# Twenty-eight more softmax tiles transposed by the DMA crossbar, a convolution without a pass for its middle tap, and a list scheduler that holds the DMA queue only while it issues

## The chip, the cores and the metric

One core of a Trainium2 chip. The metric is the device time of one execution in microseconds; lower is better. Engines: PE multiplies matrices, DVE, ACT and POOL work element by element, SP issues nearly all DMAs, in its program's order. Every engine runs its instructions in order and waits at semaphores.

## The reference

Attention with a threshold, then a gated feed-forward network, all in float32. B = 8 batches, 8 heads, S = 576 positions, head dimension 64; the model has 512 columns, the hidden layer 1024.

```python
scores = scale * np.matmul(q, k.transpose(0, 1, 3, 2))
thresh = np.max(scores, axis=-1, keepdims=True) - tau
scores = np.where(scores >= thresh, scores, -1000000000.0)
...
attn = attn / (np.sum(attn, axis=-1, keepdims=True) + 1e-09)
return np.matmul(attn, v).astype(np.float32)
...
h = np.maximum(x @ w_in, 0.0)
...
for k in range(K):
    conv_out += conv_w[k][None, None, :] * hp[:, k:k + S, :]
gate = 1.0 / (1.0 + np.exp(-conv_out))
return (h * gate @ w_out).astype(np.float32)
```

x has the heads of one position side by side. The convolution runs over positions, with three taps for each hidden column.

## The kernel before

**Tiles and stages.** The 576 positions of a batch are five tiles, four of 128 rows and one of 64. Two heads make a pair, four pairs a batch; a batch is cut into two chunks of tiles, (0, 1) and (2, 3, 4). A *unit* is one tile of one pair: 160 in all, in the order batch, chunk, pair, tile. Odd pairs take a chunk's tiles in reverse. For each unit and head PE computes the scores (`ps_s`, 128 x 576), DVE the row maximum into `few`, ACT the exponential into `em`, DVE the mask and its sum, and POOL multiplies by the inverse sum (`em`, line 602). The product with v needs the probabilities transposed. A full tile has 9 blocks of 128 x 128 (two heads of 576 columns): PE transposes 4, 4 and 1 of them into `ps_t` (line 661), the last in a group `odd` shared by the tiles of a pair, and ACT copies them to `eT` (line 656). When the last tile of an odd pair is there, `attend` multiplies `eT` of both pairs with v into `pa` (lines 716 and 725); in the first batch each pair does so alone.

**The crossbar path.** Where `crossed(i, t)` is true, `cross` does the transposing without PE: ACT and POOL split the 32-bit words of `em` into two halves of 16 bits (`parts`), SP stores them to DRAM (`rows`), and two transposing DMAs bring them back into `eT`. Before, that is the first tile of the even pairs of each chunk, except in batch 0 (`plain`): 28 tiles.

**The feed-forward part.** When the four pairs of a chunk are there, `mm1(c, f, xs)` computes 128 of the hidden columns over a chunk's positions (8 calls a chunk, 128 in all): 12 matmuls into `ph`; ACT's ReLU into `hp`, halved; the middle tap `cw[1] * hp` into `t`, on ACT for three calls of four and on POOL for the fourth (`TAP`); two DVE instructions that add the outer taps; ACT's tanh; DVE's gate `(t + 1) * hp`; and the split into the ring `g` for float32 products, which `mm2` multiplies with w_out into `po` (line 826) for 128 positions at a time.

**What sets the order.** Nothing runs where it stands in the code. `op(engine, ns, fn, ...)` puts each instruction on a list with a duration, a rank and what it reads and writes, and `Plan.run` plays the list with these durations, `LATENCY` behind each (`late` is added to it), and the counts of buffers: on each free engine the ready instruction of the lowest rank goes next, and the instructions are emitted in that order. For some operations an engine is chosen among `other`. So the durations given to SP decide where its DMAs stand among each other and how early the instructions that need them stand on other engines.

Of the kernel before, what the change touches and what calls it, by code (L numbers as in the profile page):

```python
# [10 lines left out]
F32 = mybir.dt.float32  # L11
# [4 lines left out]
AF = mybir.ActivationFunctionType  # L16
ALU = mybir.AluOpType
# [4 lines left out]
AHEAD = {'s': 6.25, 's4': 7.75, 't': 3.5, 'a': 3.5, 'prep': 4.25, 'w': 2.5, 'load': 7.75}  # L22
# [6 lines left out]

NEAR = 8  # L30
PIECES = 12
TAP = ('act', 'pool', 'act', 'act')
LOW = ('pool', 'pool')
HPB = 3
MOE = (2, 2)
# [16 lines left out]

FAR = 3
EMS = 5

KEEP = {'rows': 2.304, 'cols': 1.613, 'turn': 3.226, 'full': 2.304}

# [192 lines left out]
def tile_tau_attention_gated_ffn(  # L250
# [49 lines left out]
    def const(name, shape, dtype):  # L300
        return plan.buf(cpool, name, 1, shape, dtype, name)
# [30 lines left out]
    def sp(n):  # L332
        return 2.6 * n

    def act(n, psum=False):
        return n * 0.833 + (58 if psum else 95)

    def dve(n, fixed=65):
        return n * 1.07 + fixed
# [4 lines left out]
    def pool1(n):  # L344
        return n * 0.9 + 225
# [69 lines left out]
    cw = const("cw", [P, n3], F32)  # L415
    cwl = const("cwl", [P, n3], F32)

    def load_conv():
        split(conv_w, n3, "stage_c", lambda: cw[:], lambda: cwl[:], (cw, 0), (cwl, 0))
        op("dve", 100, lambda: nc.vector.tensor_tensor(cw[:], cw[:], cwl[:], op=ALU.add), w=[(cw, 0)], r=[(cwl, 0)])  # L420

    w1 = [const(f"w1{i}", [P, NCB, DF], F32R) for i in "hl"]
    w2 = [const(f"w2{i}", [P, NFB, DO], F32R) for i in "hl"]
# [22 lines left out]
    def plain(b):  # L446
        return b == 0
# [39 lines left out]

    def prep_k(b, p, ks):

        a = AHEAD["prep"]  # L490
        xk = plan.buf(wk, "xk", 2, [P, S + D], F32, f"xk_{b}_{p}")
        op("sp", sp(S), lambda: nc.sync.dma_start(xk[:, :S], kt[b, p]), w=[(xk, 0), (xk, 1)], ahead=a + 2)
        op("act", act(S), lambda: nc.scalar.activation(xk[:, :S], xk[:, :S], AF.Copy, scale=0.125), w=[(xk, 0), (xk, 1)], ahead=a)
        op("act", act(S), lambda: nc.scalar.activation(ks[:, 0], xk[:, :S], AF.Copy), w=[(ks, (0, 0)), (ks, (0, 1))], r=[(xk, 0)], ahead=a)
        op(
            "pool", pool(S), lambda e: subtract(e, xk[:, :S].bitcast(F32R), xk[:, :S], ks[:, 0].bitcast(F32)),
            w=[(xk, 0), (xk, 1)], r=[(ks, (0, 0)), (ks, (0, 1))], ahead=a, other=[("dve", dve(S))], port=True
        )
        halves(ks, (ks, Later(lambda: ks[:, 0], S), ((0, 0), (0, 1))), [((1, 1), 1)], a)
        halves(ks, (xk, Later(lambda: xk[:, :S].bitcast(F32R), S), (0, 1)), [((1, 0), 1), ((0, 1), 0)], a)  # L500

    def prep_q(i, b, p, q1, q2):

        w, o = QW, chunks[pairs[i][0]].new[0]
        xq = plan.buf(wk, "xq", 2, [P, w], F32, f"xq_{i}")
        a = AHEAD["prep"]
        op("sp", sp(w), lambda: nc.sync.dma_start(xq[:], qt[b, p, :, o:o + w]), w=[(xq, 0)], ahead=a + 2)
        op("act", act(w), lambda: nc.scalar.activation(q1[:, 0], xq[:], AF.Copy), w=[(q1, (0, 0)), (q1, (0, 1))], r=[(xq, 0)], ahead=a)
        op(
            "pool", pool(w), lambda e: subtract(e, q2[:, 0], xq[:], q1[:, 0].bitcast(F32)),  # L510
            w=[(q2, (0, 0)), (q2, (0, 1))], r=[(xq, 0), (q1, (0, 0)), (q1, (0, 1))], ahead=a, other=[("dve", dve(w))], port=True
        )
        for q in (q1, q2):
            halves(q, (q, Later(lambda q=q: q[:, 0], w), ((0, 0), (0, 1))), [((1, 1), 1), ((1, 0), 1), ((0, 1), 0)], a)

    def load_v(i, b, p):
        vt = plan.buf(wk, "v", 2, [P, NBLK, D], F32, f"v_{i}")
        op("sp", sp(NBLK * D), lambda: nc.sync.dma_start(vt[:], vc[b, p]), w=[(vt, 0)], ahead=AHEAD["prep"])
        return vt

    def unit(u, k, q1, q2, o, n):
# [90 lines left out]

    def crossed(i, t):
        c, p = pairs[i]
        return not plain(chunks[c].b) and p % 2 == 0 and t == order(i)[0]

    def cross(u, em, eT, off):

        parts = plan.buf(wk, "parts", 2, [P, 2, 2 * S], U16, f"parts_{u}")
        rows = plan.buf(far, "rows", FAR, [2 * P, 2 * S], U16, f"rows_{u}")  # L620
        a = AHEAD["s"]
        for j in range(2):
            def part(e, j=j):
# [9 lines left out]
        op(  # L633
            "sp", sp(2 * S), lambda: nc.sync.dma_start(rows[:].rearrange("(q two) k -> q two k", two=2), parts[:]),
            w=[(rows, 0)], r=[(parts, 0), (parts, 1)], ahead=a
        )
        for j in range(2):
            def turn(j=j):
                nc.sync.dma_start_transpose(eT[:].bitcast(U16)[:, off // D + j], rows[j * P:(j + 1) * P, :])
# [101 lines left out]
    def mm1(c, f, xs):  # L741
# [25 lines left out]
        def relu():  # L767
            nc.scalar.activation(hp[:, o:o + an], ph[:, :an], AF.Relu, scale=0.5)  # L768

        def tap0(e):  # L770
            if e == "act":
                nc.scalar.activation(t[:, :kn], hp[:, 1:kn + 1], AF.Copy, scale=cw[:, 3 * f + 1:3 * f + 2])  # L772
            else:
                engines[e].tensor_scalar(
                    t[:, :kn], hp[:, 1:kn + 1], cw[:, 3 * f + 1:3 * f + 2], 1.0, op0=ALU.mult, op1=ALU.mult
                )

        op("pool", 36, edge, w=[(hp, 1)])
        op("act", act(an, True), relu, w=[(hp, 0)], r=[(ph, 0)])
        choice = {"pool": pool1(kn), "dve": dve(kn / 2, 75), "act": act(kn)}  # L780
        home = TAP[f % len(TAP)]
        op(
            home, choice[home], tap0, w=[(t, 0)], r=[(hp, 0), (cw, 0)], port=True,
            other=[(e, ns) for e, ns in choice.items() if e != home]
        )
        for k in (0, 2):
            def tap(k=k):
                nc.vector.scalar_tensor_tensor(  # L788
                    t[:, :kn], hp[:, k:kn + k], cw[:, 3 * f + k:3 * f + k + 1], t[:, :kn], op0=ALU.mult, op1=ALU.add
                )  # L790

            op("dve", dve(kn, 150), tap, w=[(t, 0)], r=[(hp, 0), (hp, 1), (cw, 0)], port=True)

        def gate():
            nc.vector.scalar_tensor_tensor(t[:, :kn], t[:, :kn], 1.0, hp[:, 1:kn + 1], op0=ALU.add, op1=ALU.mult)  # L795

        op("act", act(kn), lambda: nc.scalar.activation(t[:, :kn], t[:, :kn], AF.Tanh), w=[(t, 0)])  # L797
        op("dve", dve(kn), gate, w=[(t, 0)], r=[(hp, 0)], port=True)

        at = (b * S + k0) % RING  # L800
# [16 lines left out]
    def mm2(m):  # L817

        gh, gl = ring
        at = m * P % RING  # L820
        po = plan.buf(ps_w, "ps_w", 2, [P, 512], F32, f"po_{m}")
        ot = plan.buf(wk, "ot", 2, [P, DO], F32, f"ot_{m}")
        for f in range(NFB):
            def mm(f=f):
                for i, (x, w) in enumerate(((gh, w2[0]), (gl, w2[0]), (gh, w2[1]))):
                    nc.tensor.matmul(  # L826
                        po[:], lhsT=x[:, f, at:at + P], rhs=w[:, f, :],
                        start=(f == 0 and i == 0), stop=(f == NFB - 1 and i == 2)
                    )
# [165 lines left out]
```

## Time and profile before

| | |
|---|---|
| median of 3 runs | 921.64 us (921.11 to 922.96) |
| the profiled execution: time, span | 924.3 us, 922.5 us |
| mean granted TensorE clock | 0.992 |
| PE busy in its span | 883.3 us, 6056 matmuls and transposes |
| DVE, ACT, POOL busy | 755.5, 699.5, 616.9 us |
| DMA | 137.0 MB, queue 1 takes 54.7% of 16 engines' time |

Busy times of the engines overlap. A row of the groups gives an instruction's line, engine and operation, what it writes and reads, the shapes and the count, then the busy time, the mean duration in ns, and how long the engine stood idle ahead of it, with who ended that. The chain follows back from the last instruction whatever released each step.

### The profile page before, as it was taken

The page shows a single profiled execution, that of the slowest core. Times are in us where ns is not written, and L with a number is a line of the kernel's source. Part 1 is how long each engine was busy: PE and PEld are TensorE (multiplying, and loading weights), DVE is VectorE, ACT ScalarE, POOL GpSimd, SP SyncE. Part 2 cuts the span into 40 slices and gives each one's busy share as a digit, 9 for nine tenths or more (in the row PEclk, how much of TensorE's full clock was granted, in tenths as well). Part 3 has the DMA queues.
Part 4 walks back from the last instruction along what each step waited for, and adds up shares of the span by engine and source line. Part 5 has one row for each costly group of instructions (what it writes and reads, how often), then busy time and mean ns, then how long its engine had stood idle before and what let it go on. Part 6 is the DMA issues. An engine that isn't in the chain of part 4 may idle for free.

```text
span 922.5 us, 19191 instructions
## 1 busy us (share of the span) xinstructions
PE 883.3 (96%) x6056; PEld 708.5 (77%) x6056; DVE 755.5 (82%) x1871; ACT 699.5 (76%) x1547; POOL 616.9 (67%) x1053
## 2 busy tenths in 40 slices
PE   5989799999999999999999999999899999999998
PEld 3546578778788787888788788887788888877896
DVE  5899799968789878896988779897888879988543
ACT  5778688768778787887878687787868868876753
POOL 3566777757768676785868767776676758775422
PEclk9999899999999999999999999999999999999999
DMA  6554357457675566547675376556757278653000
GB/s 211 174 172 133 82 149 186 128 157 162 173 186 140 153 189 189 121 121 195 177 189 153 104 193 165 137 150 169 194 150 183 75 192 195 175 135 101 24 24 34
DMA packets 148260, 137.02 MB, mean 149 GB/s; under 512 B 85312, under 2 KB 116288, under 8 KB 148160
## 3 DMA queue, kind: packets, MB, share of 16 engines
q1 hardware_dynamic: 147296, 133.90, 54.7%
q10 hardware_dynamic: 864, 1.90, 0.7%
q8 instruction: 49, 0.80, 0.4%
q14 instruction: 51, 0.42, 0.2%
HBM read 58.88 MB, written 25.95 MB: 92 GB/s over the span
## 4 chain that ended last, share of the span: by engine, by line
PE 73%; DVE 9%; POOL 6%; ACT 6%; issue 3%; DMA 3%; SPq 0%; ACTq 0%; POOLq 0%; DVEq 0%
PE po L826 20%; PE ph L753 13%; PE pa L725 13%; PE ps_s L549 11%; PE ps_t L661 10%; POOL em L602 3%; PE ps_s L542 3%; DVE em L569 3%; DVE few L557 2%; PE pa L716 2%; ACT eT L656 1%; DVE t L788 1%; ACT em L566 1%; PE pw_stage L399 1%; DMA stage<-in_w_in_dram 1%
## 5 line engine op out<-in xcount | busy, mean ns | idle before, releaser
L602 POOL TENSOR_SCALAR em<-em,few 128x576 f32<-128x576 f32 x286 | 262.7, 926 | 35.0 <-DVE few L593 21.7
L569 DVE SCALAR_TENSOR_TENSOR em<-ps_s,few,em 128x576 f32<-128x576 f32 x288 | 229.9, 813 | 26.4 <-ACT em L566 15.2
L557 DVE TENSOR_REDUCE few<-ps_s 128x1 f32<-128x576 f32 x288 | 210.1, 750 | 43.4 <-PE ps_s L549 28.0
L753 PE MATMUL ph<-x,w1h 128*128 128x322 f32 (+1 forms) x1024 | 239.0, 306 | 3.4 <-ACT hp L768 2.5
L566 ACT ACTIVATE em<-ps_s,few 128x576 f32<-128x576 f32 x288 | 208.1, 742 | 41.0 <-DVE few L557 36.8
L656 ACT ACTIVATE eT<-ps_t 128x512 f32<-128x512 f32 (+2 forms) x360 | 167.9, 487 | 30.4 <-PE ps_t L661 27.6
L788 DVE SCALAR_TENSOR_TENSOR t<-hp,cw,t 128x255 f32<-128x255 f32 (+1 forms) x256 | 160.0, 634 | 33.6 <-ACT t L772 28.6
L753 PEld LDWEIGHTS ph<-x,w1h 128*128 128x128 f32 x1024 | 174.4, 190 | 10.2 <-ACT hp L768 4.7
L661 PE MATMUL ps_t<-ident,em 128*128 128x128 f32 x1060 | 158.3, 279 | 9.7 <-POOL em L602 4.4
L549 PE MATMUL ps_s<-ks,q 128*128 128x288 f32 x896 | 152.8, 305 | 6.2 <-issue 3.8
L661 PEld LDWEIGHTS ps_t<-ident,em 128*128 128x128 f32 x1060 | 125.6, 143 | 36.9 <-POOL em L602 14.9
L753 PE MATMUL ph<-x,w1l 128*128 128x322 f32 (+1 forms) x512 | 151.6, 296 | 0.0
L549 PEld LDWEIGHTS ps_s<-ks,q 128*128 128x128 f32 x896 | 129.4, 189 | 23.3 <-issue 13.3
L329 POOL TENSOR_TENSOR gl<-t,gh 128x255 fp32r<-128x255 f32 (+9 forms) x192 | 121.0, 644 | 32.6 <-ACT gh L805 32.3
L725 PE MATMUL pa<-eT,v 128*64 128x320 f32 (+1 forms) x1024 | 132.2, 410 | 0.0
L826 PE MATMUL po<-w2h,gh 128*128 128x512 f32 x288 | 119.8, 416 | 0.6 <-ACT hp L768 0.6
L725 PEld LDWEIGHTS pa<-eT,v 128*64 128x64 f32 x1024 | 70.4, 137 | 58.9 <-issue 15.4
L826 PE MATMUL po<-w2l,gh 128*128 128x512 f32 x288 | 113.8, 395 | 0.0
L826 PE MATMUL po<-w2h,gl 128*128 128x512 f32 x288 | 113.4, 394 | 0.0
L753 PEld LDWEIGHTS ph<-x,w1l 128*128 128x128 f32 x512 | 97.1, 190 | 0.4
L795 DVE SCALAR_TENSOR_TENSOR t<-t,hp 128x321 f32<-128x321 f32 (+1 forms) x128 | 74.5, 584 | 12.6 <-ACT t L797 11.5
L563 POOL TENSOR_SCALAR few<-few,ntau 128x1 f32<-128x1 f32 x96 | 34.5, 360 | 67.0 <-DVE few L557 51.7
(72 smaller groups left out, 1106.7 us busy)
## 6 DMA issues: line engine op xcount, KB each, us to landing
q<-q SPq DMA_DIRECT2D x336, 64.0 KB, 2.1
v<-in_vc_dram SPq DMA_DIRECT2D x64, 288.0 KB, 3.6
rows<-parts SPq DMA_DIRECT2D x28, 576.0 KB, 3.4
k<-in_kp_dram SPq DMA_DIRECT2D x35, 320.0 KB, 3.8
out_dram<-ot SPq DMA_DIRECT2D x36, 256.0 KB, 2.3
xk<-in_kt_dram SPq DMA_DIRECT2D x28, 288.0 KB, 3.2
ks<-xk SPq DMA_DIRECT2D x56, 144.0 KB, 2.6
xq<-in_qt_dram SPq DMA_DIRECT2D x56, 128.0 KB, 2.5
```

Source lines behind the costliest of these rows:

```text
L329: engines[e].tensor_tensor(dst, x, y, op=ALU.subtract)
L549: nc.tensor.matmul(ps[:, c, :CH], lhsT=q[:, h, o:o + n], rhs=k[:, h, c * CH:(c + 1) * CH], start=(i == 0), stop=(i == 1))
L557: nc.vector.tensor_reduce(few[:rows, nm], ps[:rows, :, :CH], op=ALU.max, axis=mybir.AxisListType.XY, negate=True)
L566: nc.scalar.activation(view(), ps[:rows, :, :CH], AF.Exp, bias=few[:rows, nm])
L569: nc.vector.scalar_tensor_tensor(view(), ps[:rows, :, :CH], few[:rows, th], view(), op0=ALU.is_ge, op1=ALU.mult, accum_out=few[:rows, total])
L602: engines[e].tensor_scalar(sl, sl, by, to, op0=ALU.mult, op1=ALU.add)
L656: "act", act(w, True), lambda dst=dst, src=src: nc.scalar.activation(dst(), src(pt), AF.Copy),
L661: nc.tensor.transpose(out=pt[:, at:at + P], in_=em[:, int(b * P):int(b * P) + P], identity=ident[:])
L725: nc.tensor.matmul(pa[j * D:(j + 1) * D, :w], lhsT=vt[:, blk, :], rhs=eT[:, :w // D, blk, :], start=False, stop=(r == 3))
L753: nc.tensor.matmul(ph[:, :an], lhsT=w1[w][:, cb, fs], rhs=xs[cb][:, h, :an], start=(cb == 0 and i == 0), stop=(cb == NCB - 1 and i == 2))
L788: nc.vector.scalar_tensor_tensor(t[:, :kn], hp[:, k:kn + k], cw[:, 3 * f + k:3 * f + k + 1], t[:, :kn], op0=ALU.mult, op1=ALU.add)
L826: nc.tensor.matmul(po[:], lhsT=x[:, f, at:at + P], rhs=w[:, f, :], start=(f == 0 and i == 0), stop=(f == NFB - 1 and i == 2))
```

## The change

There are three parts, and the order of the whole program follows from them.

1. `crossed` takes the first full tile of every pair in each chunk but those of batch 0: 56 tiles. In odd pairs, whose order is reversed, that is tile 1 of the first chunk and tile 3 of the second.
2. The pass for the middle tap is gone. Once, from the loaded taps, 14 small DVE instructions make `cr`, the outer taps divided by the middle one, and `cm`, whose first row is the middle tap, moved a little where it is next to zero. Each call then has two DVE instructions, `hp[0] * cr0 + hp[1]` and `hp[2] * cr1 + t`, and tanh takes `cm` as its scale.
3. In the list, a load or a store holds SP for 450 ns, and the rest of its old duration is added to the time until its data is there (`put`). The small copies between partitions (`halves`) hold SP for 550 ns, a transposing DMA for 1400 with 700 behind it.

```diff
-TAP = ('act', 'pool', 'act', 'act')
...
+CROSS = (1, 1)
...
+    def put(fn, n, issue=450, **kw):
+        op("sp", issue, fn, late=max(sp(n) - issue, 0), **kw)
...
     def load_conv():
...
-        op("dve", 100, lambda: nc.vector.tensor_tensor(cw[:], cw[:], cwl[:], op=ALU.add), w=[(cw, 0)], r=[(cwl, 0)])
+        v = nc.vector
+
+        def steps():
+            yield v.tensor_tensor, (cw[:], cw[:], cwl[:]), dict(op=ALU.add)
+            for i, k in enumerate((0, 2)):
+                yield v.tensor_scalar, (cr[:, i], taps(k), -1.0, None), dict(op0=ALU.mult)
+                yield v.tensor_tensor, (cr[:, i], cr[:, i], taps(k)), dict(op=ALU.max)
...
+            yield v.scalar_tensor_tensor, (cm[:, 0], cm[:, 0], 2.0, taps(1)), dict(op0=ALU.mult, op1=ALU.add)
+            yield v.reciprocal, (cm[:, 1], cm[:, 0]), {}
+            for i, k in enumerate((0, 2)):
+                yield v.tensor_tensor, (cr[:, i], taps(k), cm[:, 1]), dict(op=ALU.mult)
...
             op(
-                "sp", max(sp(n) / 2, 360),
+                "sp", 550,
...
-        op("sp", sp(S), lambda: nc.sync.dma_start(xk[:, :S], kt[b, p]), w=[(xk, 0), (xk, 1)], ahead=a + 2)
+        put(lambda: nc.sync.dma_start(xk[:, :S], kt[b, p]), S, w=[(xk, 0), (xk, 1)], ahead=a + 2)
...
-        op("sp", sp(w), lambda: nc.sync.dma_start(xq[:], qt[b, p, :, o:o + w]), w=[(xq, 0)], ahead=a + 2)
+        put(lambda: nc.sync.dma_start(xq[:], qt[b, p, :, o:o + w]), w, w=[(xq, 0)], ahead=a + 2)
...
-        op("sp", sp(NBLK * D), lambda: nc.sync.dma_start(vt[:], vc[b, p]), w=[(vt, 0)], ahead=AHEAD["prep"])
+        put(lambda: nc.sync.dma_start(vt[:], vc[b, p]), NBLK * D, w=[(vt, 0)], ahead=AHEAD["prep"])
...
-        return not plain(chunks[c].b) and p % 2 == 0 and t == order(i)[0]
+        return not plain(chunks[c].b) and t in [x for x in order(i) if TILES[x][1] == P][:CROSS[p % 2]]
...
-        op(
-            "sp", sp(2 * S), lambda: nc.sync.dma_start(rows[:].rearrange("(q two) k -> q two k", two=2), parts[:]),
+        put(
+            lambda: nc.sync.dma_start(rows[:].rearrange("(q two) k -> q two k", two=2), parts[:]), S,
...
-            op("sp", 1350, turn, w=[(eT, (off, j))], r=[(rows, 0)], ahead=a, late=400)
+            op("sp", 1400, turn, w=[(eT, (off, j))], r=[(rows, 0)], ahead=a, late=700)
...
-        def tap0(e):
-            if e == "act":
-                nc.scalar.activation(t[:, :kn], hp[:, 1:kn + 1], AF.Copy, scale=cw[:, 3 * f + 1:3 * f + 2])
...
-        for k in (0, 2):
-            def tap(k=k):
-                nc.vector.scalar_tensor_tensor(
-                    t[:, :kn], hp[:, k:kn + k], cw[:, 3 * f + k:3 * f + k + 1], t[:, :kn], op0=ALU.mult, op1=ALU.add
-                )
+        for j, k in enumerate((0, 2)):
+            def tap(j=j, k=k):
+                y = t[:, :kn] if j else hp[:, 1:kn + 1]
+                nc.vector.scalar_tensor_tensor(t[:, :kn], hp[:, k:kn + k], cr[:, j, f:f + 1], y, op0=ALU.mult, op1=ALU.add)
...
-        op("act", act(kn), lambda: nc.scalar.activation(t[:, :kn], t[:, :kn], AF.Tanh), w=[(t, 0)])
+        op("act", act(kn), lambda: nc.scalar.activation(t[:, :kn], t[:, :kn], AF.Tanh, scale=cm[:, 0, f:f + 1]), w=[(t, 0)], r=[(cr, 0)])
...
-        op("sp", sp(DO), lambda: nc.sync.dma_start(tokens[m * P:(m + 1) * P, :], ot[:, :DO]), r=[(ot, 0)])
+        op("sp", 450, lambda: nc.sync.dma_start(tokens[m * P:(m + 1) * P, :], ot[:, :DO]), r=[(ot, 0)])
```

What moves is seen at pair 9, the first odd pair with a crossing: batch 1, tile 1 as unit 22 (crossed now), then tile 0 as unit 23. The last number in a name counts the tiles in the order of emission, and the numbers ahead of it are unit, pair or chunk. First PE before, from unit 23's transposes to the product with v of pairs 8 and 9:

```order
L661 MATMUL ps_t_23_4_1674<-ident_83,em_23_1584 128x128 x4
L661 MATMUL ps_t_23_8_1684<-ident_83,em_23_1584 128x128
L661 MATMUL ps_t_23_8_1684<-ident_83,em_22_1518 128x128
L753 MATMUL ph_1_4_1690<-x_4_330,w1h_233 128x322
...
L753 MATMUL ph_1_4_1690<-x_6_559,w1h_233 128x322
L716 MATMUL pa_8_1711<-eT_8_1546,v_8_1330 64x256 x2
L716 MATMUL pa_9_1714<-eT_9_1612,v_9_1540 64x256 x2
```

And the same place after:

```order
L694 MATMUL ps_t_23_4_1707<-ident_83,em_23_1599 128x128 x4
...
L694 MATMUL ps_t_23_8_1728<-ident_83,em_23_1599 128x128
...
L786 MATMUL ph_1_5_1748<-x_7_740,w1h_235 128x322
...
L786 MATMUL ph_1_6_1783<-x_7_740,w1h_235 128x322
L749 MATMUL pa_8_1810<-eT_8_1565,v_8_1279 64x256 x2
L749 MATMUL pa_9_1813<-eT_9_1714,v_9_1519 64x256 x2
```

Unit 22's transposes are gone, its block of the odd group too, and between the last transpose and the product stand two more hidden column blocks (`ph_1_5`, `ph_1_6`) and the scores of unit 25. SP's queue at this place before:

```order
L482 DMA ks_1_3_1576<-xk_1_3_1479 64x576
L482 DMA q1_11_1603<-q1_11_1603 64x256 x2
L482 DMA q2_10_1484<-q2_10_1484 64x256
L482 DMA q2_11_1620<-q2_11_1620 64x256
L482 DMA ks_1_3_1576<-xk_1_3_1479 64x576
L482 DMA q2_11_1620<-q2_11_1620 64x256
L507 DMA xq_12_1706<-in_qt_dram 128x256
L482 DMA q1_11_1603<-q1_11_1603 64x256
L456 DMA k_12_1725<-in_kp_dram 128x640
```

And after:

```order
L515 DMA ks_1_3_1549<-xk_1_3_1479 64x576 x2
L515 DMA q1_11_1616<-q1_11_1616 64x256
L667 DMA rows_22_1656<-parts_22_1626 128x2304
L515 DMA q1_11_1616<-q1_11_1616 64x256
L515 DMA q2_11_1649<-q2_11_1649 64x256 x2
L540 DMA xq_13_1685<-in_qt_dram 128x256
L489 DMA k_13_1695<-in_kp_dram 128x640
L672 DMA_TRANSPOSE eT_9_1714<-rows_22_1656 128x9x128 x2
L515 DMA q1_11_1616<-q1_11_1616 64x256
L515 DMA q2_11_1649<-q2_11_1649 64x256
```

The store and the two transposing DMAs of unit 22 have come in among the copies of q for pair 11, whose second halves now stand behind the transposes; the loads of q and k are a pair further ahead. Last, ACT in the hidden layer of the same chunk before:

```order
L772 ACTIVATE t_1_0_1626<-hp_1_0_1352,cw_465 128x321
L768 ACTIVATE hp_1_1_1499<-ph_1_1_1572 128x322
L768 ACTIVATE hp_1_2_1538<-ph_1_2_1616 128x322
L797 ACTIVATE t_1_0_1626<-t_1_0_1626 128x321
L656 ACTIVATE eT_9_1612<-ps_t_23_0_1653 128x2x256
L772 ACTIVATE t_1_2_1672<-hp_1_2_1538,cw_465 128x321
```

And after:

```order
L801 ACTIVATE hp_1_1_1553<-ph_1_1_1589 128x322
L322 ACTIVATE parts_22_1626<-em_22_1539 128x1152
L815 ACTIVATE t_1_0_1607<-t_1_0_1607,cm_478 128x321
L801 ACTIVATE hp_1_2_1555<-ph_1_2_1618 128x322
L823 ACTIVATE gh_1070<-t_1_0_1607 128x257
```

The middle taps (line 772) are gone, tanh (797, now 815) reads `cm`, and the split of unit 22 stands where two copies to `eT` stood.

More of the change, by code (lines that the diff above doesn't have):

```diff
@@ L416, in tile_tau_attention_gated_ffn, with taps, ratios @@
     cwl = const("cwl", [P, n3], F32)
+    cr = const("cr", [P, 2, NFB], F32)
+    cm = const("cm", [P, 2, NFB], F32)
+    def taps(k):
+        return cw[:].rearrange("p (f k) -> p k f", k=3)[:, k]
     def load_conv():
         split(conv_w, n3, "stage_c", lambda: cw[:], lambda: cwl[:], (cw, 0), (cwl, 0))
-        op("dve", 100, lambda: nc.vector.tensor_tensor(cw[:], cw[:], cwl[:], op=ALU.add), w=[(cw, 0)], r=[(cwl, 0)])
+        v = nc.vector
[4 more added lines that the diff above has]
+                yield v.tensor_tensor, (cr[:, i], cr[:, i], taps(k)), dict(op=ALU.max)
+            yield v.tensor_tensor, (cm[:, 0], cr[:, 0], cr[:, 1]), dict(op=ALU.max)
+            yield v.tensor_scalar, (cm[:, 0], cm[:, 0], 2.0 ** -60, 2.0 ** -100), dict(op0=ALU.mult, op1=ALU.max)
+            yield v.tensor_scalar, (cm[:, 1], taps(1), -1.0, None), dict(op0=ALU.mult)
+            yield v.tensor_tensor, (cm[:, 1], cm[:, 1], taps(1)), dict(op=ALU.max)
+            yield v.tensor_tensor, (cm[:, 1], cm[:, 1], cm[:, 0]), dict(op=ALU.is_lt)
+            yield v.tensor_tensor, (cm[:, 0], cm[:, 0], cm[:, 1]), dict(op=ALU.mult)
+            yield v.scalar_tensor_tensor, (cm[:, 0], cm[:, 0], 2.0, taps(1)), dict(op0=ALU.mult, op1=ALU.add)
+            yield v.reciprocal, (cm[:, 1], cm[:, 0]), {}
+            for i, k in enumerate((0, 2)):
+                yield v.tensor_tensor, (cr[:, i], taps(k), cm[:, 1]), dict(op=ALU.mult)
+        def ratios():
+            for f, a, kw in steps():
+                f(*a, **kw)
+        op("dve", 1100, ratios, w=[(cw, 0), (cr, 0)], r=[(cwl, 0)])
     w1 = [const(f"w1{i}", [P, NCB, DF], F32R) for i in "hl"]
@@ L768, in relu @@
             nc.scalar.activation(hp[:, o:o + an], ph[:, :an], AF.Relu, scale=0.5)
[L770 to L776 removed]
         op("pool", 36, edge, w=[(hp, 1)])
         op("act", act(an, True), relu, w=[(hp, 0)], r=[(ph, 0)])
[L780 to L785, printed above, removed]
[L786 to L792 removed]
+        for j, k in enumerate((0, 2)):
+            def tap(j=j, k=k):
+                y = t[:, :kn] if j else hp[:, 1:kn + 1]
+                nc.vector.scalar_tensor_tensor(t[:, :kn], hp[:, k:kn + k], cr[:, j, f:f + 1], y, op0=ALU.mult, op1=ALU.add)
+            op("dve", dve(kn, 150), tap, w=[(t, 0)], r=[(hp, 0), (hp, 1), (cr, 0)], port=True)
         def gate():
             nc.vector.scalar_tensor_tensor(t[:, :kn], t[:, :kn], 1.0, hp[:, 1:kn + 1], op0=ALU.add, op1=ALU.mult)
[L797 removed]
+        op("act", act(kn), lambda: nc.scalar.activation(t[:, :kn], t[:, :kn], AF.Tanh, scale=cm[:, 0, f:f + 1]), w=[(t, 0)], r=[(cr, 0)])
         op("dve", dve(kn), gate, w=[(t, 0)], r=[(hp, 0)], port=True)
```

## The prediction

> **What bounds the kernel.** I read the page's busy times and slices first, then the chain, then a table of busy time over the stretch that holds all seven batches the change touches.
>
> ```profile
> span 922.5 us, 19191 instructions
> PE 883.3 (96%) x6056; PEld 708.5 (77%) x6056; DVE 755.5 (82%) x1871; ACT 699.5 (76%) x1547; POOL 616.9 (67%) x1053
> ...
> PE   5989799999999999999999999999899999999998
> ...
> PE 73%; DVE 9%; POOL 6%; ACT 6%; issue 3%; DMA 3%; SPq 0%; ACTq 0%; POOLq 0%; DVEq 0%
> ...
> 0.00:60.00 60.00, 47.32 (x231) 25.25 (x232) 45.38 (x110) 41.19 (x83) 29.20 (x60) 0.97 0.57 181
> ...
> 120.00:862.00 742.00, 727.63 (x5152) 600.85 (x5148) 631.91 (x1594) 582.34 (x1289) 526.37 (x891) 1.00 0.61 159
> ```
>
> In a windows row stand the length, then PE, PEld, DVE, ACT and POOL busy, the granted clock and the DMA engines' share. From 120 to 862 us PE is busy 727.6 of 742 us, DVE 85%, ACT 78%, POOL 71%, and PE holds 73% of the chain. So I take PE's order of work as the bound there. Busy PE time overlaps; what one instruction costs is the distance of two starts, which the chain's rows show where equal instructions run on:
>
> ```profile
> 154.17 1.26 PE ps_s L549 x8
> 155.43 2.25 PE ph L753 x15
> ...
> 429.89 0.76 PE ps_t L661 x7
> ...
> 431.37 0.44 PE ps_t L661 x4
> ```
>
> A transpose costs 0.76/7 = 0.109 us, a hidden-layer matmul 0.150, a score matmul 0.157. Against this reading stands the Trainium skill, "Perfetto Trace Analysis", section "Identifying the Most-Contended Engine": matmul busy time is no measure of PE's headroom, the share of weight loads is. By it PE would be at 600.9/742 = 81%, below DVE's 85%, and the change would relieve the wrong engine; that result is rival D below. The chain's 73% on PE against 9% on DVE speaks against it here.
>
> **Part 1, 28 more tiles by the crossbar.** Removed from PE: 9 transposes of each tile, 252 of 1060. The costs of everything that goes and comes, group by group (busy, mean ns):
>
> ```profile
> L661 PE MATMUL ps_t<-ident,em 128*128 128x128 f32 x1060 | 158.3, 279 | 9.7 <-POOL em L602 4.4 <-ACT eT L656 3.2 <-POOL hp L763 1.1
> L656 ACT ACTIVATE eT<-ps_t 128x512 f32<-128x512 f32 x232 | 134.7, 599 | 28.6 <-PE ps_t L661 26.9
> L322 ACT ACTIVATE parts<-em 128x1152 uint16<-128x1152 uint16 x28 | 32.7, 1167 | 3.5 <-POOL em L602 3.5
> L324 POOL COPY parts<-em 128x1152 uint16<-128x1152 uint16 x28 | 32.4, 1158 | 0.3
> L563 DVE TENSOR_SCALAR few<-few,ntau 128x1 f32<-128x1 f32 x171 | 32.3, 209 | 0.7
> L563 POOL TENSOR_SCALAR few<-few,ntau 128x1 f32<-128x1 f32 x96 | 34.5, 360 | 67.0 <-DVE few L557 51.7
> L656 ACT ACTIVATE eT<-ps_t 128x256 f32<-128x256 f32 x36 | 14.0, 389 | 0.8 <-PE ps_t L661 0.7
> L656 ACT ACTIVATE eT<-ps_t 128x128 f32<-128x128 f32 x28 | 8.1, 290 | 0.1
> ```
>
> PE: 252 x 0.109 = **-27.5 us**, all in the PE-bound stretch. The other end is the mean busy time, 158.3/1060 = 0.149 us, so -37.6; I take the step, since it is what the next instruction waits for.
> ACT: 56 copies of 512 columns go (-56 x 0.599 = -33.5), 28 copies shrink from 256 to 128 columns (-28 x 0.099 = -2.8), 28 splits come (+28 x 1.167 = +32.7): -3.6.
> POOL: 28 splits, +32.4; 13 threshold computations move to DVE (11, +2.3 us) and ACT (2), -4.7.
>
> SP and the DMA engines get 28 stores and 56 crossbar transfers:
>
> ```profile
> L639 SPq DMA_TRANSPOSE eT<-rows x56: 1258/1507/2287, 138.0 to 849.8; - x56
> ...
> DMA to landing us min/median/max: 3.6/4.1/6.0
> L634 SPq DMA_DIRECT2D rows<-parts x28: 343/357/1352, 133.8 to 843.9; - x28
> ...
> DMA to landing us min/median/max: 2.8/3.4/6.2
> 133.82 0.35 SPq L634 DMA_DIRECT2D rows<-parts  x1
> ...
> 138.00 3.01 SPq L639 DMA_TRANSPOSE eT<-rows  x2
> q1 hardware_dynamic: 147296, 133.90, 54.7%
> rows<-parts SPq DMA_DIRECT2D x28, 576.0 KB, 3.4
> SPq L518 <- PE pa L725: 57.5, 30, 13.1
> ```
>
> SP: 56 x 1.507 + 28 x 0.357 = +94 us of issuing. It is covered as long as SP has waits such as the 57.5 us before loads of v; what stands behind a transfer, the q and ks copies of coming tiles, goes out 3.0 us later. Bytes: each tile is written once and read back once, 28 x 2 x 0.59 = 33 MB. Queue 1 took 54.7% of 922.5 us for 133.9 MB, 3.77 us a MB, so +125 us of all 16 engines; their share of the stretch rises from 0.61 to (453 + 125)/714 = 0.81.
>
> The price is lateness. Of the first crossing the store starts at 133.82, the transfers at 138.00, and the second lands about 1.5 + 4.1 us later: 9.8 us in all. In the new order of pair 9 there stand, from that store to the product with v, 16 score matmuls, 39 of the hidden layer and 9 transposes: 2.5 + 5.9 + 1.0 = 9.4 us, up to 10.7 if the nine matmuls just ahead of the store still lie behind it. The even pair before has some 19 us, as the 28 crossings of before have 15 to 32. Counted so, with each kind's usual step, the 28 odd pairs have 6.9 to 16.1 us of PE work there, median 10.4; where that is under 9.8 the lacks add up to 12 us. Who waits is PE itself, in order, with the scores of the next pair behind it. Before, such waits are mostly for copies of ACT, seven, and none for a transfer:
>
> ```profile
>   ACT eT L656: 5.6, 7
> ```
>
> PE's steps between are longer than bare (14.4 us of idle stand in the stretch already), which hides some; nothing of it could be below zero. Ends: 0, and +38 if every crossing took 11.5 us. I take **+8**, two thirds of the 12. The Trainium skill, "Advanced Engine Details and Errata", section "X-Bar Transpose (TRN2)", says that transposing DMAs are as fast as regular ones. This trace does not quite agree: half the bytes of the store take 4.1 us against 3.4. By the rule the sum would be some 5 us lower.
>
> **Part 2, no middle tap.** The middle tap's product goes; the outer taps are divided by it beforehand and tanh multiplies it back in.
>
> ```profile
> L772 ACT ACTIVATE t<-hp,cw 128x321 f32<-128x321 f32 x48 | 27.2, 567 | 2.6 <-POOL gl L329 1.3
> L772 ACT ACTIVATE t<-hp,cw 128x255 f32<-128x255 f32 x48 | 24.4, 509 | 3.0 <-POOL gl L329 1.6 <-POOL hp L765 0.9
> L774 POOL TENSOR_SCALAR t<-hp,cw 128x321 f32<-128x321 f32 x16 | 10.5, 655 | 12.6 <-ACT hp L768 11.1 <-ACT gh L805 0.7
> L774 POOL TENSOR_SCALAR t<-hp,cw 128x255 f32<-128x255 f32 x16 | 9.1, 568 | 6.0 <-ACT hp L768 5.2 <-DMA q<-q 0.2
> L797 ACT ACTIVATE t<-t 128x255 f32<-128x255 f32 x64 | 26.4, 413 | 8.5 <-DVE t L788 8.3
> L805 ACT ACTIVATE gh<-t 128x255 fp32r<-128x255 f32 x40 | 16.5, 414 | 5.4 <-DVE t L795 5.4
> L788 DVE SCALAR_TENSOR_TENSOR t<-hp,cw,t 128x321 f32<-128x321 f32 x128 | 80.7, 638 | 13.2 <-ACT t L772 11.3 <-POOL t L774 1.1 <-POOL hp L765 0.4
> L590 DVE TENSOR_SCALAR few<-few 128x2 f32<-128x2 f32 x81 | 14.9, 184 | 0.0
> DVE t L788 <- ACT t L772: 28.6, 13, 10.1
> ```
>
> ACT: -27.2 - 24.4 = -51.6. But tanh now takes its scale from a tile. A copy of 255 columns with a fixed scale takes 414 ns, one with a scale from a tile 509: +95 ns, and if tanh pays the same, 128 x 0.095 = +12.2. With part 1 ACT loses 43 us of 699.5. POOL: -19.6, with part 1 +8 of 616.9. Both engines have room, so only their places on the chain count: ACT's 6% (55 us) x 43/699.5 = -3.4 at most, 0 at least; I take **-1.5**. POOL's share moves by +0.7, which I leave out. The first tap reads hp twice where it read hp and t; shape and kind stay, so 638 ns stays. DVE's 13 waits for the middle tap (28.6 us) end earlier, but now end at the ReLU, 0.5 us ahead; without PE behind them they bring nothing.
> Once, 14 DVE instructions on 128x8 work out the ratios: 14 x 0.184 = 2.6 us in the first 60 us, where DVE is busy 45.4 and PE waits for others too. With the 11 thresholds, and 4 guards that move with them (4 x 0.184), +5.6 at most, 0 at least; I take **+1**.
>
> **Part 3, the list's SP times.** Loads hold SP for 450 ns and land later by the difference, copies of q and ks are 550 ns: no instruction changes, only the order. The measured issue (0.36 for a store, 1.51 for a transfer) is nearer to the new numbers, so I cost it at nothing beyond the waits above.
>
> **Sum.** The profiled execution took 924.3 us, 1.8 around its span, 2.7 above the median of 921.64. 924.3 - 27.5 + 8 - 1.5 + 1 = 904.3, less 2.7: **901.6 us**, 2.2% faster.
>
> **Rivals.** (B) The relief of ACT and the shorter path from ReLU to gate also close PE's idle, and the attention waits are absorbed: up to 924.3 - 37.6 - 3.4 - 2.7 = 880.6; a middle value is 887. For it: 28.6 us of DVE waits at the middle tap. Against: PE idles only 14.4 us in the stretch.
> (C) The odd pairs' legs run at 10.6 us, the lacks are some 23 us: 916.6, still faster.
> (D) DVE bounds: its work is unchanged but for at most 5.6 us, so 922, no change. For it 85% busy, near 89% when PE shortens; against, its 9% of the chain.
> (E) Slower: PE waits at the odd pairs' products with v because the crossings run late under 81% DMA load. The lacks at legs of 11.3 us are 34, of 12.3 us 53: 927.6 and 946.6; I price it at 930. It decides from 28 us, legs of 10.9, 1.1 above the first crossing. For it: the longest landings, 6.0 and 6.2 us, are 1.9 and 2.8 over their medians. Against: the medians, and that PE's real steps are longer than bare.
>
> **Chances.** Forecast (890 to 912) 0.58, B 0.12, C 0.11, D 0.06, E 0.13. What differs by under 0.2% a measurement here cannot tell from no change: faster 0.81, same 0.06, slower 0.13. From 884 to 921 are left out about 0.05 below and 0.15 above.
>
> **What would show it.** In the profile after: 808 transposes at the same step, PE still at 97% or more between 120 and the end of the attention; tanh at about 510 ns for 255 columns; the wait of the product with v on a transfer from the crossbar, in sum 5 to 12 us; DMA share near 0.8 there. I am wrong if that wait exceeds 28 us, if DVE rises over 90% with PE under 95%, or if landings of the transfers pass 5 us in the median.

## The result, and the profile after

| | before | after |
|---|---|---|
| median of 4 runs each, on one chip | 921.38 us | 960.28 us |
| range of the runs | 920.05 to 922.96 | 958.78 to 962.14 |
| ratio to before, 95% interval | | 1.0422 [1.0406, 1.0437] |
| the profiled execution's span | 922.5 us | 957.0 us |
| mean granted TensorE clock | 0.992 | 0.975 |

4.2% slower, where 2.2% faster was forecast. First the page of the kernel after: busy times (PEld is PE's loading of weights), PE's slices and its granted clock in tenths (9 is 90% or more), and the shares of the chain of work that ended last. Then one row of the table of busy time by stretch, for the same 742 us as in the prediction (length, PE, PEld, DVE, ACT and POOL busy, granted clock, DMA share, GB/s), and PE's transposes and the new tanh from the groups.

```profile
span 957.0 us, 18802 instructions
PE 876.4 (92%) x5804; PEld 691.2 (72%) x5804; DVE 774.8 (81%) x1900; ACT 671.1 (70%) x1425; POOL 623.4 (65%) x1032
...
PE   5899899897999997998999989998899989999998
...
PEclk9999799999999998998999999999999999999999
...
PE 44%; DMA 17%; DVE 13%; ACT 10%; SPq 6%; issue 5%; POOL 5%; ACTq 0%; POOLq 0%; DVEq 0%
```

```profile
120.00:862.00 742.00, 687.34 (x4679) 556.79 (x4679) 618.96 (x1534) 533.52 (x1137) 513.57 (x840) 0.98 0.76 196
```

```profile
L694 PE MATMUL ps_t<-ident,em 128*128 128x128 f32 x808 | 125.0, 281 | 21.3 <-DVE x L768 14.6 <-DVE few L626 2.3 <-ACT eT L689 2.1
L815 ACT ACTIVATE t<-t,cm 128x255 f32<-128x255 f32 x64 | 32.4, 506 | 13.8 <-DVE t L808 11.5 <-DVE few L626 1.6 <-DVE few L623 0.5
```

The transposes went as planned, from 1060 to 808. But between 120 and 862 us PE is busy 687.3 of 742 us, 93% where it was 98%. No other engine has become the bound: DVE is at 83%, ACT at 72%. In the chain PE's share falls from 73% to 44%, while DMA rises from 3% to 17%, ACT from 6% to 10%, and SP's queue from 0 to 6%. The chain now runs through transfers.

PE's idle time in the span was 922.5 - 883.3 = 39.2 us and is 957.0 - 876.4 = 80.6, so +41.4, and busy PE time fell by only 6.9 although transposes worth 27.5 us by their step are gone. That sums to the +34.5 us of span. An estimate from the clock covers most of the missing 20 us: the share not granted times the span is 0.008 x 922.5 = 7.4 us before and 0.025 x 957.0 = 23.9 after, 16.5 more (the clock has three decimals, so each is good to 0.5 us).

Who stands and for what is in the view of waits (engine and line, what released it: us in sum, times, longest), of ACT, then DVE, PE and SP. Of before, the largest waits of ACT on a load were 3.0 us for xk and 2.2 for q, and PE hardly ever waited on a transfer. First the rows of before:

```profile
ACT x L732 <- PE pa L725: 41.9, 38, 1.7
DVE x L735 <- ACT x L732: 23.9, 30, 1.7
ACT xk L493 <- DMA xk<-in_kt_dram: 3.0, 4, 1.3
ACT q L471 <- DMA q<-in_qd_dram: 2.2, 3, 0.8
```

And of after:

```profile
ACT x L765 <- PE pa L758: 52.9, 37, 5.2
ACT q L501 <- DMA q<-in_qd_dram: 24.4, 14, 3.8
...
ACT xk L526 <- DMA xk<-in_kt_dram: 17.3, 11, 3.3
```

```profile
DVE x L768 <- ACT x L765: 56.7, 37, 4.9
```

```profile
PE ps_t L694 <- DVE x L768: 14.6, 11, 2.8
...
PE ps_s L582 <- DMA q<-q: 7.5, 5, 2.3
PE ps_s L582 <- DMA ks<-xk: 6.4, 3, 3.0
...
PE pa L749 <- ACT eT L689: 5.0, 4, 2.4
...
PE pa L749 <- DMA q<-q: 4.0, 2, 2.4
PE pa L749 <- DMA eT<-rows: 3.5, 4, 2.6
```

SP's own largest waits for PE are those before loads of v (before: 57.5 us):

```profile
SPq L551 <- PE pa L758: 45.8, 14, 13.2
```

ACT stands 24.4 + 17.3 us at instructions that only prepare coming pairs (lines 501 and 526), because their loads are not there. The last row of PE is the wait that the prediction priced at +8: 3.5 us. PE's largest wait, 14.6 us, is for DVE's `x`, the low half of the attended values. DVE stands for ACT's high half (56.7 us, before 23.9), and that for the product `pa` on PE (52.9, longest 5.2; before 41.9, longest 1.7). So a late product can come back to PE by way of ACT and DVE.

One place shows how such a wait reaches PE. The timeline after (start, length, engine, what), SP's queue first, then ACT, then PE:

```profile
666.41 3.20 SPq L672 DMA_TRANSPOSE eT<-rows  x2
...
671.32 1.23 SPq L525 DMA_DIRECT2D xk<-in_kt_dram  x1
```

```profile
674.39 0.61 ACT L689 ACTIVATE eT<-ps_t 128x512 f32<-128x512 f32 x1
678.27 0.68 ACT L526 ACTIVATE xk<-xk 128x576 f32<-128x576 f32 x1 [3.28 <-DMA xk<-in_kt_dram]
678.86 0.58 ACT L689 ACTIVATE eT<-ps_t 128x512 f32<-128x512 f32 x1
...
682.10 0.22 ACT L689 ACTIVATE eT<-ps_t 64x64 f32<-64x64 f32 x1
```

```profile
679.50 0.76 PE L749 MATMUL pa<-eT,v 64*64 64x320 f32 x4 [0.67 <-ACT eT L689]
682.63 0.76 PE L749 MATMUL pa<-eT,v 64*64 64x320 f32 x4 [2.38 <-ACT eT L689]
683.32 6.22 PE L758 MATMUL pa<-eT,v 128*64 128x320 f32 x32
```

Two crossbar transfers hold SP for 3.20 us, a load of v, a store and a copy follow, and the load of `xk` goes out at 671.32. It lands about 7 us later (its median is 3.6, so it was also slow on its way). ACT, which runs in order, stands 3.28 us at the scaling of `xk`. The copies to `eT` for the current pair are queued behind that, done late, and PE waits for them. Then 32 products with v take 6.22 us; before, 32 of them took 4.46. The table of busy time shows why:

```profile
670.00:679.00 9.00, 8.65 (x67) 7.99 (x65) 7.23 (x21) 4.89 (x10) 4.74 (x7) 1.00 0.84 240
679.00:683.00 4.00, 1.13 (x8) 0.42 (x8) 1.84 (x5) 3.94 (x10) 2.49 (x2) 1.00 0.90 191
683.00:690.00 7.00, 7.00 (x40) 3.39 (x37) 3.27 (x11) 4.37 (x11) 3.53 (x7) 0.76 0.91 277
```

From 679 to 683 us, while PE waits for ACT's copies, it is busy 1.13 of 4 us, and in the next 7 us the granted clock is 0.76. So a stall can be paid twice. The Trainium skill, "TensorE: Matmul & The Clock Gate", sections "Part 1: The HAM clock gate" and "HAM oscillation", says that a monitor of PE's activity halves its clock after an idle window of some 3.4 us, and that waits on DMAs can set this off again and again. This trace agrees that the clock falls behind a stall, but it took less than a wholly idle window: the longest wait here was 2.38 us.

### The profile page after: what moved, and what is told of

Read it like the earlier page. It is cut to its first block, busy times and chain, and to the rows that moved or that the text cites. A ratio compares the mean times of both kernels' runs of the same rounds, so it can differ in the third digit from the quotient of the medians.

```text
span 957.0 us, 18802 instructions
## 1 busy us (share of the span) xinstructions
PE 876.4 (92%) x5804; PEld 691.2 (72%) x5804; DVE 774.8 (81%) x1900; ACT 671.1 (70%) x1425; POOL 623.4 (65%) x1032
## 4 chain that ended last, share of the span: by engine, by line
PE 44%; DMA 17%; DVE 13%; ACT 10%; SPq 6%; issue 5%; POOL 5%; ACTq 0%; POOLq 0%; DVEq 0%
PE po L844 12%; PE ph L786 10%; PE pa L758 7%; PE ps_s L582 6%; PE ps_t L694 5%; DVE em L602 3%; DMA q<-in_qd_dram 3%; DVE few L590 3%; SPq L672 3%; DMA q<-q 3%; DMA xk<-in_kt_dram 3%; DMA rows<-parts 3%; ACT em L599 3%; PE ps_s L575 2%; ACT eT L689 2%
## 5 line engine op out<-in xcount | busy, mean ns | idle before, releaser
L635 POOL TENSOR_SCALAR em<-em,few 128x576 f32<-128x576 f32 x286 | 257.1, 907 | 39.5 <-DVE few L626 31.3
L582 PE MATMUL ps_s<-ks,q 128*128 128x288 f32 x896 | 160.4, 309 | 22.3 <-DMA q<-q 7.5
L689 ACT ACTIVATE eT<-ps_t 128x512 f32<-128x512 f32 (+3 forms) x304 | 133.4, 457 | 18.8 <-PE ps_t L694 16.8
L694 PE MATMUL ps_t<-ident,em 128*128 128x128 f32 x808 | 125.0, 281 | 21.3 <-DVE x L768 14.6
L758 PE MATMUL pa<-eT,v 128*64 128x320 f32 (+1 forms) x1024 | 140.2, 428 | 0.0
L694 PEld LDWEIGHTS ps_t<-ident,em 128*128 128x128 f32 x808 | 96.9, 144 | 45.9 <-issue 20.5
L758 PEld LDWEIGHTS pa<-eT,v 128*64 128x64 f32 x1024 | 73.7, 144 | 65.2 <-issue 24.7
L844 PE MATMUL po<-w2h,gh 128*128 128x512 f32 x288 | 117.2, 407 | 0.7 <-ACT ot L851 0.4
L808 DVE SCALAR_TENSOR_TENSOR t<-hp,cr 128x321 f32<-128x321 f32 (+1 forms) x128 | 83.4, 654 | 15.8 <-ACT hp L801 15.6
L815 ACT ACTIVATE t<-t,cm 128x321 f32<-128x321 f32 (+1 forms) x128 | 68.2, 534 | 29.2 <-DVE t L808 18.3
```

What stands on the lines that cost most here:

```text
L582: nc.tensor.matmul(ps[:, c, :CH], lhsT=q[:, h, o:o + n], rhs=k[:, h, c * CH:(c + 1) * CH], start=(i == 0), stop=(i == 1))
L635: engines[e].tensor_scalar(sl, sl, by, to, op0=ALU.mult, op1=ALU.add)
L689: "act", act(w, True), lambda dst=dst, src=src: nc.scalar.activation(dst(), src(pt), AF.Copy),
L694: nc.tensor.transpose(out=pt[:, at:at + P], in_=em[:, int(b * P):int(b * P) + P], identity=ident[:])
L758: nc.tensor.matmul(pa[j * D:(j + 1) * D, :w], lhsT=vt[:, blk, :], rhs=eT[:, :w // D, blk, :], start=False, stop=(r == 3))
L808: nc.vector.scalar_tensor_tensor(t[:, :kn], hp[:, k:kn + k], cr[:, j, f:f + 1], y, op0=ALU.mult, op1=ALU.add)
```

## The experiments

All are stated against the runs of the kernel before in the same batch (921.4, 922.1, 920.7, 920.3 or 921.4 us), with the 95% interval of the ratio. The theories are named by letters in the expectations: **A**, what the prediction counted, PE waiting at the odd pairs' products because crossings come late. **L**, those late crossings with the halved clock behind them. **S**, the list's new SP times order the DMAs badly. **T**, the tap's removal crowds DVE. **R**, the new times leave the list no reserve: half the transfers land later than it assumes, and engines that run in order stand at them. **H**, the load on the DMA engines. **I**, the time that the crossbar transfers hold SP. **X**, the crossbar itself delays other transfers.

**Each part alone.** e1: before, with part 1 only.

```diff
+CROSS = (1, 1)
...
-        return not plain(chunks[c].b) and p % 2 == 0 and t == order(i)[0]
+        return not plain(chunks[c].b) and t in [x for x in order(i) if TILES[x][1] == P][:CROSS[p % 2]]
```

> Only the crossings are changed: 56 tiles instead of 28, the middle tap and the list's old SP times stay. Theory L (the 28 new crossings arrive late, PE waits at products and scores and its clock is halved): about 955 us, as the whole change. Rival S (the new SP times put the DMAs in a bad order): the crossings alone save their transposes, about 900 us.

e2: before, with part 2 only (the diff of `cr`, `cm`, the two taps and tanh).

> Only the middle tap's pass is gone. Theory L and rival S: 917 to 922 us, since ACT and POOL are not the bound. Rival T (the tap's removal lets the hidden layer's work crowd DVE): 935 us or more.

e3: before, with part 3 only (`put`, 550 for the copies, 1400 and 700 for the transfers).

> Only the list's SP times are changed, 28 crossings and the middle tap stay. Theory L: 918 to 926 us, the order of the DMAs is about as good as before. Rival S: 945 to 960 us, nearly the whole loss, with scores that wait for the small copies of q and ks.

e4: the whole change without the new crossings.

```diff
-CROSS = (1, 1)
+CROSS = (1, 0)
```

> The whole change without the 28 new crossings (only even pairs cross, as before). Theory L: 912 to 922 us. Rival S: 940 us or more.

| | median us | ratio [95%] | span | PE busy | clock |
|---|---|---|---|---|---|
| e1 | 969.4 | 1.0520 [1.0488, 1.0552] | 966.1 | 883.6 | 0.972 |
| e2 | 922.4 | 1.0013 [0.9996, 1.0030] | 919.5 | 879.9 | 0.991 |
| e3 | 934.2 | 1.0134 [1.0107, 1.0160] | 934.0 | 883.7 | 0.995 |
| e4 | 932.5 | 1.0116 [1.0090, 1.0141] | 930.8 | 880.8 | 0.994 |

T falls: without the middle tap the time is the same. Part 3 costs 10 to 12 us by itself, with no new transfer (e4 over e2, and e3 over before), so S or R holds for that share. That is under 2%, but clear of the noise. Neither e3 nor e4 lies in a range that was expected: both fall between theirs. e1 is slower than either of its two. The new crossings cost 960.3 - 932.5 = 28 us with the new times and 47 us with the old ones. In e1 the rows are others: ACT and PE wait little for loads, but ACT stands for DVE and PE for ACT (the rows below; before 36.8 and 2.5 us). So its 47 us are for the most part not loads held back on SP. The list holds SP there for 3.0 us at each store, which measured 0.36 before; e10 below bears on that:

```profile
ACT em L567 <- DVE few L558: 71.1, 80, 4.2
...
PE ph L754 <- ACT hp L769: 21.6, 14, 3.3
```

The whole change, with parts 2 and 3, is 9 us faster than e1, while part 3 harms where part 1 is absent. In e3, one more row shows what it does:

```profile
ACT q L472 <- DMA q<-in_qd_dram: 17.4, 12, 2.7
```

**More reserve in the list.** e5: after, with 1 us more behind every DMA in the list. e6: the same without the new crossings.

```diff
-LATENCY = {"pe": 210.0, "act": 145.0, "dve": 110.0, "pool": 75.0, "sp": 2000.0}
+LATENCY = {"pe": 210.0, "act": 145.0, "dve": 110.0, "pool": 75.0, "sp": 3000.0}
```

> The whole change, but the list counts 3000 ns instead of 2000 from the end of each SP hold until the data is there. Theory R (the new SP times left no reserve: half of all DMAs land later than the list assumes, and ACT and PE stand in order behind them): 925 to 943 us. Rival H (the transfers' load on the DMA engines is the cost, whatever the order): 950 us or more.

> As the kernel without the 28 new crossings (932.5 us), with 3000 ns of latency in the list. Theory R: 917 to 925 us, the waits of ACT on loads of q and xk fall from some 30 us to under 10. Rival H: unchanged, 929 to 936, since the load is that of the kernel before.

e7: after, with 2 us more behind the crossbar transfers alone, so that the list puts the products with v later.

```diff
-            op("sp", 1400, turn, w=[(eT, (off, j))], r=[(rows, 0)], ahead=a, late=700)
+            op("sp", 1400, turn, w=[(eT, (off, j))], r=[(rows, 0)], ahead=a, late=2700)
```

> The whole change; only the crossbar transfers' own data is planned 2 us later. Rival A (what the prediction counted: PE waits at the products with v of odd pairs): 925 to 935 us. Theory R: 948 to 960 us, since the loads of q, k and xk and the small copies stay as late as they were.

e5 took 942.7 us, 1.0248 [1.0224, 1.0271], 17.6 less than after; e6 927.4, 1.0080 [1.0048, 1.0112], 5.1 less than e4; e7 956.1, 1.0388 [1.0335, 1.0442], 4 less than after. The gain of e7 is not clear of the noise, since its interval holds that of after; the intervals of e6 and e4 overlap too. Two more microseconds for the crossings bring at most a quarter of what one more brings for all DMAs. So A and L are small, and R carries more. e5 lies at the edge of R's range. In e6, R's range is missed by 2.4 us, and ACT still waits 18 us for loads of q and xk, where under 10 were expected. In e7 PE's sum of waits on crossings is 1.2 us, and ACT still stands for the loads:

```profile
ACT q L501 <- DMA q<-in_qd_dram: 30.7, 15, 4.3
```

**Load on the DMA engines, or SP's time?** These two keep every instruction of after in its place, and change only what the transfer from DRAM to `eT` is and which halves the split writes. e8 copies plainly, e9 copies in pieces of 256 bytes. The data is not transposed in either, and the split writes the high halves twice, so the output is not the attention's.

```diff
-                nc.sync.dma_start_transpose(eT[:].bitcast(U16)[:, off // D + j], rows[j * P:(j + 1) * P, :])
+                nc.sync.dma_start(eT[:].bitcast(U16)[:, off // D + j], rows[j * P:(j + 1) * P, :].rearrange("p (b x) -> p b x", b=NBLK))
```

```diff
-                nc.sync.dma_start_transpose(eT[:].bitcast(U16)[:, off // D + j], rows[j * P:(j + 1) * P, :])
+                nc.sync.dma_start(eT[:].bitcast(U16)[:, off // D + j], rows[j * P:(j + 1) * P, :].rearrange("q k -> (q k)").rearrange("(b p x) -> p b x", b=NBLK, p=P))
```

> The same order on every engine, but the 112 transposing transfers are plain copies of the same bytes (the probabilities in eT are then not transposed, and the split writes the high halves twice). Rival H: under 915 us. Theory R: 920 to 940 us, as SP gets some 1.1 us back at each, which is a reserve of its own. If the transposing costs nothing: 955 to 960.

> As the plain copies (925.5 us), in pieces of 256 bytes, 1152 to a transfer, as the transposing ones have (the probabilities in eT are not transposed, and the split writes the high halves twice). Theory I (what the transposing costs is SP's issue time, 1.5 us against 0.43): 924 to 934 us, if SP issues the pieces in about 0.5 us. Rival H (many small packets load the DMA engines, and everything lands later): 945 to 960 us, at a DMA share as high as with the transposing transfers.

Line 672's transfers in after, e8 and e9, in that order (duration on SP in ns, min/median/max), and queue 1 of each (packets, MB, share of the 16 engines):

```profile
L672 SPq DMA_TRANSPOSE eT<-rows x112: 1265/1522/2614, 138.7 to 898.9; - x112
...
DMA to landing us min/median/max: 3.5/4.2/6.2
q1 hardware_dynamic: 217632, 166.94, 66.4%
```

```profile
L672 SPq DMA_DIRECT2D eT<-rows x112: 319/430/1471, 138.4 to 864.5; - x112
...
DMA to landing us min/median/max: 2.7/4.0/7.0
q1 hardware_dynamic: 101152, 166.93, 58.6%
```

```profile
L672 SPq DMA_DIRECT2D eT<-rows x112: 370/593/1687, 138.8 to 873.3; - x112
...
DMA to landing us min/median/max: 3.2/4.4/7.2
q1 hardware_dynamic: 215840, 166.93, 64.6%
```

e8 took 925.5 us, 1.0055 [1.0039, 1.0071]; e9 932.8, 1.0125 [1.0097, 1.0154]. With nearly the bytes, packets and engine share of after, and landings as late, e9 is 27.5 us faster. What differs is that 112 transfers hold SP for 0.59 us each in the median instead of 1.52: all SP's instructions in the trace sum to 587 us instead of 660 (before: 540). Whether the crossbar itself delays other transfers (X) can be read from how long those take from issue to landing. These two rows of the DMA issues (count, KB each, median us to landing) stand word for word in the pages of after and of e9:

```profile
q<-q SPq DMA_DIRECT2D x336, 64.0 KB, 2.5
xk<-in_kt_dram SPq DMA_DIRECT2D x28, 288.0 KB, 3.6
```

The loads of k and v take 3.6 and 3.7 us in both, those of q (line 490) 3.8 and 3.6. So the other transfers land no later behind their issue beside the crossbar's than beside the pieces, and X is not seen: the 27 us go with the time that the transfers hold SP, which is I. The waits fell with it: in e9 ACT stands 19.1 + 12.4 us for the loads of q and xk (after 24.4 + 17.3), and PE 12.5 us for DMAs in all (after 23.3).

e8, with half the packets, gains 7 us more, but it also takes another 62 us off SP (525), so H's packets are worth at most about 7 us. The 33 MB of the new crossings are in both and were not varied. The 27 us equal what the new crossings add over e4 (28), but the transposes worth 27.5 us are gone in e9 and present in e4, and yet the two are level.

**Is it SP's time or the crossbar?** e12 keeps the crossbar transfers and takes other work off SP: those copies of q and ks that stay in the same partitions (half equal to head) are made by an engine, 136 by POOL, 3 by ACT, 1 by DVE. e13 is e12 with e5's latency. e14 is the control: the same relief in the kernel with 28 crossings, no tap and the old holds (550 for the copies left).

```diff
+            if half == head:
+                def same(e, j=j, half=half, n=n):
+                    on = slice(half * D, (half + 1) * D)
+                    copy(e, dst[on, j, :n], view[on].bitcast(F32))
...
+                op(
+                    "pool", choice["pool"], same, w=[(dst, part)], r=[(x, parts[head])], ahead=ahead, port=True,
...
+                continue
```

> The whole change, with real crossbar transfers, but the copies of q and ks that stay on their own partitions (140 of SP's small copies, 0.55 us of issue each, 77 us) are made by POOL, now and then by ACT or DVE. Theory I (SP's issue time is the cost, some 0.25 us of time for each us on SP): 938 to 948 us. Rival X (the crossbar itself stalls other transfers, SP's time hardly matters): 955 to 962 us, or more for POOL's added 60 us.

> The same relief of SP with 3000 ns of latency in the list. Theory I with theory R (both take from the same lateness): 918 to 932 us. Rival X: 940 us or more, as with the latency alone (942.7).

> Control: 28 crossings, no middle tap, the old holds (small copies 550 ns), with the same relief of SP. Theory I: 918 to 926 us, since SP was not late in the kernel before; POOL's added work is covered. If SP's time counts at any load: under 915 us.

e12 took 948.8 us, 1.0297 [1.0250, 1.0343], 11.5 less than after, for 85 us less of SP's time (576). e13 took 931.3, 1.0113 [1.0093, 1.0132], 11.4 less than e5. e14 took 922.9, 1.0031 [1.0012, 1.0050]: at 28 crossings the relief brings nothing. e12 lies just above I's range and below X's; e13 and e14 lie in I's. So SP's time counts where 56 tiles cross and not where 28 do, as I has it. But per microsecond taken off SP e12 gains less than e9 (11.5 for 85 against 27.5 for 73), POOL carries the copies (673.9 us busy for 623.4), and queue 1's share falls too, to 60.9%. Why it gains less was not tested; e12, unlike e9, also leaves the 1.5-us transfers in the queue and changes the order. ACT's largest wait on a load stays at 23.3 us in e12.

**Other holds.** e10: before with the 56 crossings and no middle tap, the old holds for loads and copies, and a store that holds SP for 450 with 1050 behind it, a transfer for 1500 and 700. e11: after, with loads and stores holding SP for 1000.

```diff
-    def put(fn, n, issue=450, **kw):
+    def put(fn, n, issue=1000, **kw):
```

> 56 crossings and no middle tap; the list's holds of loads, small copies and output stores are the old, long ones; the crossing's store holds SP 450 ns and each transfer 1500 with 700 behind it. SP's holds then add up to more than SP really needs. Theory R: 905 to 925 us, with less than 15 us of ACT's waits on loads. Rival H: 940 us or more.

> The whole change, but put holds SP for 1000 ns instead of 450 (the data's arrival in the list stays). Theory R: 920 to 940 us, as SP's holds in the list go from under to over its real issue time. Rival H: 950 us or more.

e10 took 940.1 us, 1.0214 [1.0183, 1.0244], 20 less than after; e11 950.5, 1.0284 [1.0220, 1.0348], 10 less. In the code's own numbers all holds of SP add up to 611 us in after, for 660 us measured, and to 715 and 723 in e10 and e11; before, 681 stood for 540. Theory R failed here: both lie where the load was expected to be the cost (940 and 950 or more), not in R's ranges (though e9 speaks against the load), and in e10 ACT still waits 18.5 + 13.4 us for the loads of q and xk, where under 15 were expected. The sum of the holds does not sort the runs either: e1, whose list holds SP for 841 us where it takes 656, is the slowest, and in e4 520 stand for 535. What remains of R is that 1 us more of latency gave back 17.6 us in e5, with one reservation: e5, e6 and e10 to e14 also change the order of the whole program, so a single cause is not isolated in them as it is in e8 and e9. None of the kernels run beats the one before.

## Why the prediction was wrong, step by step

- **Transposes, -27.5 us.** The work went away, but the term assumed that a stretch bound by PE stays so. It did not: PE's idle rose by 41.4 us, and the clock, for which the prediction had no term, lost some 16.5 by the estimate above.
- **SP's +94 us of issuing at nothing, "covered as long as SP has waits".** This is the step that failed. SP's instructions went from 540 to 660 us, more than counted. The waits of 57.5 us before loads of v did not cover it. SP still stands 45.8 us there, so only some 12 us were used up. SP issues in its program's order, so a wait is cover only for what stands behind it and is not yet due, and the copies of q, `ks` and the loads behind two 1.5-us transfers were due. e9, with the same order, bytes and landings, puts the price of the transfers' long hold at about 27 us; e12 agrees in direction. The prediction had even named what "stands behind a transfer" and gave it no price.
- **Part 3 at nothing.** Wrong by 10 to 12 us (e3, e4). "No instruction changes, only the order" was taken as no cost; but the list's numbers decide how much slack each load gets. That landing times, not issue times, were the ones to check them against is suggested by e5, but not shown, since e5 changes the whole order.
- **The odd pairs' products, +8 us.** Mis-sized and minor: PE waited 3.5 us for crossings, and e7, which gives them 2 us more, gained 4 at most. The legs were read well: landings 4.2 us in the median (wrong "if over 5"), against 4.1 before.
- **Rival E** had the sign, the price 930, and 0.13, but its mechanism (late crossings under DMA load) is not the one shown, so the sign was luck. No rival spoke of loads held back in SP's queue.
- **Tanh's scale, +95 ns.** Right: 506 ns for 255 columns, 413 before. ACT lost 28.4 us, less than the 43 forecast; the relief was worth nothing (e2), where -1.5 was taken.
- **DVE, at most +5.6.** It rose by 19.3 us, from 755.5 to 774.8. The shapes stayed, but the two taps (128x321) rose from 638 ns to 667 and 664, and DVE's guards (128x2, line 586, now 619) from 263 to 402, where the prediction took the 184 of a neighbouring row. That did not set the time, since e2 with 767.2 is no slower.
- **DMA share 0.81.** 0.76 measured over the same stretch.
- **PE at 97% or more.** 93%. The stated condition, DVE over 90% with PE under 95%, did not come either: PE can lose its place without another engine taking it, by waits spread over several.

Of the 58.7 us between forecast and result, 27.5 lie between after and e9, 7 between e9 and e8, and 10 to 12 are part 3's, if these add up; e1, with 47 us for part 1 alone, says that they need not. The remaining 12 to 14 are open: why e8, with SP's time back below that of before (525 us) and the transposes gone, is still not faster than before. Its PE idle is 924.3 - 863.6 = 60.7 us, 21.5 above before; e4's, with no new crossing, is already 50.0, which puts half of it to part 3's order. The other 11 us were not tested alone. Open too is what costs 47 us in e1, where SP takes as long as in after (656 us) but its loads are hardly late.

## What to carry to other kernels

Price an in-order issuing queue as you would an engine: each long instruction delays what stands behind it, and idle time elsewhere in the queue covers only instructions that can wait. When a planner's durations are brought nearer to the issue time, check that what was in the old ones as slack (landing times that vary, a load that goes out late) is put somewhere else. Before you count work removed from the busiest engine as time won, ask which engine copies or prepares its operands in order, and what that one would stand at first.

## What the hardware showed unexpectedly

A transposing DMA of 128 rows by 1152 two-byte elements holds the issuing queue for 1.52 us in the median, a plain one of the same bytes for 0.43, one in 256-byte pieces for 0.59, while all three land in 4.0 to 4.4 us. And single waits of 1.6 to 3.0 us in a PE that is 93% busy can be enough for the clock to fall. In after the trace grants half the clock seven times between 120 and 862 us, for 3.4 or 6.8 us each, where before it was once, and PE had stood that long just ahead of each such time, or as it began. Waits of like length at 214.6, 549.5 and 662.1 us (2.4 to 2.8 us) were not followed by it. Over the span the clock went from 0.992 to 0.975, some 16.5 us by the estimate above.
